# The level products of an RWKV-7 chunk on quarters of the PE array, one matmul for each batch half

## The chip, the cores and the metric

The kernel runs on one core of one Trainium2 chip. The metric is the device time of one execution in microseconds (us). Engines are TensorE (PE, with its weight loads listed as PEld), VectorE (DVE), ScalarE (ACT), GpSimd (POOL) and SyncE (SP, which here only issues transfers).

## The reference

Two stages follow each other: a linear-attention recurrence (RWKV-7 "goose") over 4 batches, 8 heads, 768 steps and head width 40, and a SwiGLU feed-forward block over the 3072 tokens of width 320 that come out of it.

```
state = 0                                   # per batch and head, 40 x 40
for t in range(768):
    y[t]  = r[t] @ state
    Sa    = state @ a[t]
    state = state * w[t] - outer(Sa, b[t]) + outer(v[t], k[t])

x  = y as (3072, 320);  xn = x / rms(x) * rms_g
out = (silu(xn @ w_gate) * (xn @ w_val)) @ w_out        # d_ff = 1536
```

Weights and rms_g of the feed-forward block are float64 in the inputs and are narrowed on the chip; all matmuls are in float32.

## The kernel before

The sequence is cut into 24 chunks of C = 32 steps. The 32 sequences (batch x head) lie as N = 8 slots by two column halves o by two partition halves i: a half of the 128 partitions (`half(i)`, 64 rows) belongs to one batch pair, `part(o)` is the first 40 rows of a half, and NI = 16 pairs (n, i) or (o, n) share a tile.

Within a chunk the recurrence is solved by doubling levels l = 1, 2, 4, 8, 16 (`LEVELS`). For each chunk there are four functions:

- `front(c)` loads w, a, k, b and v, turns them with PE, and builds level by level the decayed products T, the keys KN[l] and the lower triangular tile LT ("gramk" matmuls with 40 rows and 64 columns of weights).
- `inverse(c)` (for c < 4 `early_inverse`) inverts the triangle, in 31 pairs of DVE operations on tiles Yi and tmp, or by halves.
- `main(c)` solves for the chunk's values ("state", "lower" matmuls), updates the state ("update"), makes the scores of r against k and b ("score"), masks them into As, and computes y: a term from the old state ("y0") and one product for each level ("level"), which `down` adds into y after a scaling with T[l].
- `feed(g)`, after every second chunk, streams the narrowed weights of the feed-forward block in 12 slices (wf) and computes "h64", "h" and "out" matmuls with 256 to 320 moving columns.

`narrow_slice` prepares these weights during the first groups.

The operations are recorded as pieces (`Plan.add`) and issued in the order of the string ORDER, a list that was searched offline: each number is a piece's place among those not issued yet, and each "-" is a filler matmul on an identity tile (`plan.warm`, 151 of them, all in the first part of the kernel). PAIRS says which of three PSUM tiles each temporary (`plan.room()`) gets. So each engine's queue is a fixed sequence, and semaphores keep the dependencies. Nearly all DVE operations have line L444, all POOL and SP transfers L483, and PE's matmuls L486 (transposes L489), since one helper issues each kind; groups are told apart by the tiles' names.

The part that is changed is in `main`. The scores `sc` come out with the partitions of both batch halves filled. For each level j the tile `As[:, j]` holds the scores of that level's steps twice, once for each batch half i, and msi is zero where the partition half is not i:

```
As[:, j, :, i]  <-  sc * msi[:, j, i]        # [P, NI, 2, 16]
level: 16 matmuls  ps[part(o), slot(n)] = KN[l][all 128 rows, 40 cols].T @ As[all 128 rows, 32 cols]
```

So one matmul contracts over all 128 partitions and makes the 16 columns of both batch halves, which the zero blocks keep apart. Levels 16 and 8 share a PSUM temporary with y0, levels 4, 2 and 1 have one of their own.

Of the kernel before, what the change touches and what calls it, by code (L numbers as in the profile page):

```python
# [17 lines left out]
P = 128  # L18
# [15 lines left out]
85 83 84 76 58 78 86 74 73 59 60 75 5 89 61 88 77 4 43 6 201 7 87 334 90 44 8 214 213 53 62 9 - - - - - - - - 93 18 10  # L34
567 335 557 11 12 13 79 14 15 94 566 80 210 16 95 558 108 17 200 - - - 97 96 19 20 100 21 2 22 101 23 98 25 568 202 24
26 107 112 57 - - - - - 102 106 111 124 27 209 122 392 103 109 52 119 113 104 54 578 569 577 155 199 125 110 105 204
120 - - - - - - 114 203 118 117 121 559 211 598 589 562 46 131 129 132 45 560 212 597 563 588 561 123 115 136 586 384
133 134 - - - - - 126 130 116 47 564 3 145 216 394 383 135 336 128 137 48 144 143 141 91 587 219 142 51 570 127 1005
565 146 138 337 55 573 579 281 393 220 582 608 571 390 234 239 607 572 583 580 380 574 251 222 38 221 609 575 581 42 -
- - - - - - - 223 82 226 339 64 379 227 338 39 81 139 224 263 149 576 238 153 56 249 247 590 206 584 228 382 237 591  # L40
593 272 40 233 232 381 154 0 593 32 139 390 204 228 591 388 234 249 247 - - 324 235 35 31 27 244 229 146 147 259 281
245 258 149 34 325 594 36 33 270 155 243 62 605 584 598 230 - 239 40 214 599 601 242 628 64 49 91 627 602 30 626 1135
600 28 48 257 603 29 241 68 150 255 65 0 1347 194 0 194 84 173 0 - - - 182 540 200 0 184 1 186 542 540 0 506 0 457 469
849 199 455 242 111 97 110 112 96 51 61 439 460 458 122 50 243 0 0 255 242 0 709 104 470 242 120 246 259 708 57 247
458 456 0 257 718 256 470 242 0 716 265 487 486 0 268 0 0 265 101 473 0 262 277 0 273 0 236 0 260 0 269 0 242 461 - -
- - - - - 237 0 240 0 278 242 252 0 242 252 0 90 0 0 98 99 246 0 0 230 440 0 230 94 93 457 440 231 - - - - - - - - -
240 441 244 0 44 0 468 440 255 0 450 468 269 469 0 257 214 439 238 213 203 0 257 203 93 449 92 0 0 234 - - - - - - - -
245 437 0 250 262 0 464 246 247 436 260 245 446 258 259 469 244 - - 255 471 465 468 470 466 0 269 215 255 478 466 93
94 264 95 96 266 97 0 97 470 1 2 98 99 0 0 96 467 97 469 98 468 251 265 99 470 100 471 101 441 102 103 258 104 105 260
106 - - - - - - - - - - - 0 106 107 471 108 0 108 502 503 472 0 108 109 110 111 0 0 0 0 0 - - 13 0 16 562 572 146 571  # L50
561 147 14 142 143 374 15 13 355 - - - 25 386 358 0 358 386 388 16 25 387 389 390 70 79 17 391 28 191 147 355 356 80
148 149 359 0 68 28 2 29 149 0 149 34 150 29 151 187 24 25 31 152 33 153 188 391 393 32 154 35 390 392 358 0 0 152 40
187 153 27 154 155 156 33 157 158 159 160 161 34 162 36 163 164 37 165 41 391 38 42 392 39 394 561 166 395 393 552 0
42 559 549 548 395 209 0 549 560 42 165 210 43 44 211 427 428 395 - - - 565 166 45 167 557 168 0 565 566 168 739 0 522
693 534 526 124 - - 0 526 124 139 0 535 681 682 579 0 535 545 547 140 536 138 141 0 547 545 555 543 578 0 558 520 567
- - - - - - 518 378 0 696 378 380 381 695 518 120 685 526 - - - - - - 522 686 379 527 382 136 530 383 554 529 121 - -
141 540 523 565 539 537 142 538 524 - - - - 145 525 148 534 149 152 154 551 535 147 555 - - 157 146 550 536 150 155
151 556 165 552 153 564 160 691 161 692 0 163 161 689 162 165 1 0 546 676 0 510 45 46 560 47 424 511 2 1 0 0 555 554
44 45 563 509 421 432 436 435 422 437 433 571 508 996 995 434 444 572 442 441 0 45 572 442 585 577 0 838 45 572 445
577 46 828 827 837 587 573 589 446 575 47 598 48 601 11 846 588 574 444 443 613 597 0 11 370 835 599 48 0 584 607 367  # L60
478 595 568 - - 35 830 594 567 820 38 36 - 476 37 571 366 570 0 605 356 433 434 435 436 120 437 0 317 318 319 320 441
321 322 323 355 456 324 458 459 442 4 357 325 457 326 327 443 328 0 443 328 329 330 331 357 0 35 0 330 2 37 450 359 3
36 358 331 332 357 333 356 0 462 330 461 464 448 331 332 468 364 447 463 31 467 476 458 333 365 334 335 0 425 439 441
302 426 436 0 6 439 2 0 435 332 2 436 443 444 0 448 332 442 334 443 333 340 449 0 32 297 329 342 330 - 3 338 33 341
334 0 332 331 0 332 293 441 0 438 0 436 293 333 336 295 337 309 438 338 1 375 342 310 365 374 515 27 292 0 362 26 28
44 339 29 34 292 27 32 338 0 646 29 34 336 32 0 439 64 315 647 646 339 440 441 63 340 0 287 413 312 313 623 12 414 314
415 315 416 608 624 32 417 480 418 625 419 420 421 316 626 638 33 0 312 417 625 418 - - - - 476 313 601 602 600 610
812 419 420 421 822 258 422 423 0 313 810 423 625 637 2 0 819 2 0 254 473 420 421 645 310 422 0 - - - - - 310 422 3
313 33 0 28 626 307 419 639 627 420 637 308 0 637 20 635 420 647 21 421 23 422 613 648 819 38 22 809 423 39 659 24 611
3 612 36 818 424 651 808 621 425 25 660 426 - 616 249 427 0 427 3 25 58 57 428 28 47 0 428 429 28 430 3 431 0 26 25  # L70
614 484 31 27 617 627 0 458 216 400 590 600 401 0 12 582 32 401 583 25 0 397 579 21 - - - - - - - - - 588 29 28 30 591
22 453 428 398 605 23 0 591 23 429 602 24 609 0 24 397 588 602 1 604 398 429 430 2 399 427 0 584 - - - - - - - - - - -
- - - 4 397 0 25 397 4 0 393 394 21 23 27 28 395 598 24 424 607 0 21 38 35 395 37 396 24 2 424 47 397 398 399 400 25
401 3 28 402 403 588 0 28 3 0 584 26 27 585 25 598 600 422 31 400 399 401 424 599 28 595 427 429 52 0 568 397 396 399
567 394 405 578 401 12 0 398 397 570 0 381 367 402 0 1 569 576 381 501 570 0 509 0 648 574 381 497 403 382 399 402 0
706 399 400 419 715 403 0 655 715 401 705 402 0 402 783 657 403 703 655 404 0 711 566 700 655 565 712 564 3 563 358 8
360 0 3 639 403 0 403 3 0 400 401 402 712 403 355 0 710 968 406 350 724 715 1134 712 711 632 716 561 976 492 416 1133
663 729 634 977 562 563 717 713 986 978 665 564 565 566 975 567 568 714 569 985 570 571 967 722 572 723 - 0 400 403
726 402 572 401 573 0 726 738 736 573 739 574 664 575 737 576 577 3 723 578 751 579 760 580 747 581 582 633 583 584 0
584 585 3 634 586 636 587 635 734 588 633 0 746 588 - - - - - 403 757 589 722 590 3 404 591 592 593 594 595 596 408  # L80
597 598 599 600 601 602 603 714 409 410 0 727 401 728 711 402 600 712 601 0 408 712 725 721 0 417 723 600 601 3 602
401 735 737 0 741 602 735 721 0 739 0 0 330 10 196 313 342 197 198 324 20 199 200 201 202 203 0 203 340 338 204 325
339 4 324 206 205 335 5 6 0 335 336 346 343 345 344 228 0 0 227 0 200 341 343 226 344 342 3 235 13 625 234 202 232 229
8 233 204 203 230 201 231 227 348 4 349 228 350 351 352 353 354 355 356 0 0 351 3 0 351 7 352 16 353 3 354 355 8 356
357 358 359 360 361 362 0 359 5 360 361 6 0 355 6 356 357 358 359 218 16 360 361 220 362 223 363 227 224 364 225 228
365 229 0 365 536 366 367 527 368 369 524 225 370 16 371 372 525 195 229 534 373 230 0 195 249 536 230 231 525 232 541
250 0 399 533 203 0 541 730 371 231 540 372 373 0 371 229 543 254 539 372 230 200 373 726 544 393 374 445 551 255 375
554 394 231 376 567 377 565 378 0 736 395 554 231 541 735 232 539 555 733 378 567 379 579 565 743 233 380 540 381 4
563 734 575 382 588 383 744 236 386 234 384 576 587 319 385 235 5 320 6 548 549 544 396 397 545 552 400 551 399 0 386
397 561 560 545 546 402 0 557 0 398 401 557 553 399 518 519 0 564 571 524 551 665 525 566 570 567 400 438 550 565 579  # L90
# [278 lines left out]
def kernel(  # L369
# [108 lines left out]
    def blank(o, value):  # L478
        plan.add("POOL", "set", lambda at: nc.gpsimd.memset(o, value), [o], [])
# [70 lines left out]
    for j, l in enumerate(LEVELS):  # L550
        for i in range(2):
            pcopy(msi[half(i), j, i:i + 1].rearrange("p n (g l) -> p n g l", l=l), side(msk[half(i)], l, 1)[:, j:j + 1])
# [495 lines left out]
```

## Time and profile before

The time before is 1067.85 us, the median of 3 runs (1063.42, 1067.85 and 1081.36). The profiled execution took 1062.36 us; its span, from the first to the last instruction, is 1060.6 us.

| engine | busy us | share of the span | instructions |
|---|---|---|---|
| PE matmuls | 1009.5 | 95% | 23406 |
| PE weight loads | 829.3 | 78% | 23406 |
| DVE | 842.3 | 79% | 2861 |
| ACT | 468.1 | 44% | 1043 |
| POOL | 309.5 | 29% | 554 |

| what the change touches | count | mean ns of one |
|---|---|---|
| level matmuls from KN tiles, 128 rows x 40 columns, 32 moving | 3072 | 205 |
| level matmuls from kbn (level 1), same shape | 768 | 205 |
| masks As on DVE, 256 elements | 144 | 416 |
| masks As on DVE, 512 elements | 42 | 683 |
| masks As on ACT, 256 elements | 12 | 473 |
| adds of a level into y on DVE, 256 elements | 119 | 420 |

A busy time is the union of an engine's instructions, which overlap on PE. A row of a group gives the operation, tiles out<-in, shapes, count, then busy us and mean ns of one, then the idle time just before them and what ended it. A float32 matmul stands as two records, a transpose as one. In the forms of PE, "128*40" is rows by columns of the weights, and behind it the output's partitions by moving columns.

### The profile page before, as it was taken

How to read it: one execution, taken by the hardware profiler on the slowest of the kernel's cores; microseconds unless marked ns; L12 is line 12 of the kernel's file. 1: busy time of each engine (PE TensorE's matmuls, PEld its weight loads, DVE VectorE, ACT ScalarE, POOL GpSimd, SP SyncE). 2: the span in 40 equal slices, each digit the busy share in tenths (PEclk: the TensorE clock that was granted, in tenths of full speed). 3: DMA queues.
4: the chain of work that ended last, by engine and by line, in shares of the span. 5: the costliest groups of instructions: out<-in, count | busy, mean ns of one | idle time of the engine just before them, and what ended most of it. 6: DMA issues, size and time to landing. Idle time of an engine off the chain costs nothing.

```text
span 1060.6 us, 53494 instructions
## 1 busy us (share of the span) xinstructions
PE 1009.5 (95%) x23406; PEld 829.3 (78%) x23406; DVE 842.3 (79%) x2861; ACT 468.1 (44%) x1043; POOL 309.5 (29%) x554
## 2 busy tenths in 40 slices
PE   7868999999999999999999999999999999999997
PEld 6767777777888778787778778787777888787875
DVE  8978878776868988898898798989889899787411
ACT  6856666643543534434443444434344443431211
POOL 8824413120532241241233241340331331110000
PEclk9777998999999999999999999999999999999999
DMA  9965458766565483655565555574555555443252
GB/s 168 216 155 133 77 127 207 211 123 178 127 140 126 106 173 96 150 134 125 123 155 129 135 132 114 122 160 119 137 126 126 138 137 138 100 132 102 80 162 68
DMA packets 172457, 143.35 MB, mean 135 GB/s; under 512 B 125504, under 2 KB 143872, under 8 KB 172224
## 3 DMA queue, kind: packets, MB, share of 16 engines
q1 hardware_dynamic: 153856, 116.96, 42.9%
q0 software_dynamic: 16192, 22.64, 12.1%
q8 instruction: 184, 3.01, 1.2%
q10 hardware_dynamic: 2176, 0.33, 0.3%
q14 instruction: 49, 0.40, 0.1%
HBM read 123.86 MB, written 15.99 MB: 132 GB/s over the span
## 4 chain that ended last, share of the span: by engine, by line
PE 72%; DVE 8%; DMA 4%; ACT 3%; issue 3%; POOL 2%; SPq 1%; DVEq 0%; ACTq 0%; POOLq 0%
PE ps L486 50%; PE po L486 13%; PE ps L489 8%; DMA wf<-sW 2%; DVE LT L444 1%; DVE y L444 1%; DVE tmp L444 1%; POOL kbn L483 1%; DVE Yi L444 1%; DVE K L444 1%; SPq L483 1%; DMA sY<-Yi 1%; ACT VU L467 1%; PE po L1015 0%; DVE Ab L444 0%
## 5 line engine op out<-in xcount | busy, mean ns | idle before, releaser
L486 PE MATMUL ps<-xg,wf 128*128 128x256 f32 (+1 forms) x1728 | 353.5, 390 | 4.0 <-DVE xg L444 2.0
L486 PEld LDWEIGHTS ps<-xg,wf 128*128 128x128 f32 (+1 forms) x1728 | 261.4, 188 | 57.2 <-issue 15.0
L486 PE MATMUL po<-wf,hT 128*128 128x320 f32 x576 | 183.1, 449 | 0.1
L464 ACT ACTIVATE sg<-ps 128x256 f32<-128x256 f32 x144 | 53.6, 382 | 228.2 <-PE ps L486 224.9
L444 DVE TENSOR_TENSOR tmp<-Yi,M 128x60 f32<-128x60 f32 (+24 forms) x620 | 130.7, 211 | 19.1 <-DMA M<-sB 5.9
L444 DVE TENSOR_TENSOR Yi<-Yi,tmp 128x60 f32<-128x60 f32 (+24 forms) x620 | 129.7, 209 | 12.7
L483 POOL DMA_DIRECT2D VU<-in_v_dram x92 | 53.2, 584 | 274.1 <-PE ps L486 141.8
L486 PEld LDWEIGHTS po<-wf,hT 128*128 128x128 f32 x576 | 102.5, 191 | 35.7 <-issue 4.1
L444 DVE TENSOR_TENSOR hT<-ps,sg 128x256 f32<-128x256 f32 x144 | 59.7, 420 | 67.2 <-ACT sg L464 66.4
L444 DVE TENSOR_TENSOR K<-K,T 128x512 f32<-128x512 f32 (+1 forms) x192 | 93.4, 496 | 8.3 <-PE ps L486 5.8
L486 PEld LDWEIGHTS ps<-Ab,K 40*64 40x64 f32 x4608 | 77.2, 138 | 28.1 <-issue 10.5
L467 ACT COPY K<-K 128x256 f32<-128x256 f32 (+1 forms) x168 | 71.7, 443 | 58.4 <-PE ps L486 39.2
L486 PE MATMUL ps<-Ab,K 40*64 40x56 f32 x4608 | 87.2, 224 | 9.7 <-issue 3.8
L444 DVE TENSOR_TENSOR As<-ps,msi 128x256 f32<-128x256 f32 (+1 forms) x186 | 78.9, 476 | 14.4 <-PE ps L486 13.8
L467 ACT COPY KN<-ps 128x640 f32<-128x640 f32 x96 | 66.1, 690 | 53.5 <-PE ps L489 23.3
L483 POOL DMA_DIRECT2D kbn<-in_b_dram x92 | 53.3, 583 | 96.7 <-PE ps L486 94.3
L486 PEld LDWEIGHTS ps<-As,KN 128*40 128x40 f32 x3072 | 66.5, 124 | 15.7 <-issue 10.4
L483 POOL DMA_DIRECT2D kbn<-in_k_dram x92 | 53.6, 585 | 82.7 <-PE ps L486 82.6
L486 PE MATMUL ps<-As,KN 128*40 128x32 f32 x3072 | 73.2, 205 | 3.1 <-issue 2.5
L483 POOL DMA_DIRECT2D wn<-in_w_dram x92 | 51.6, 567 | 62.7 <-DVE tmp L444 24.1
L444 DVE TENSOR_TENSOR y<-y,ps 128x256 f32<-128x256 f32 x119 | 50.0, 420 | 16.2 <-PE ps L486 13.7
L444 DVE COPY_PREDICATED LT<-near,ps 128x384 f32<-128x384 uint32 (+2 forms) x72 | 52.2, 725 | 2.6 <-PE ps L486 2.0
(133 smaller groups left out, 1546.0 us busy)
## 6 DMA issues: line engine op xcount, KB each, us to landing
wf<-sW SPq DMA_DIRECT2D x144, 480.0 KB, 3.9
M<-sB SPq DMA_DIRECT2D x80, 128.0 KB, 4.1
rn<-in_r_dram SPq DMA_DIRECT2D x24, 160.0 KB, 5.4
sW<-ex SPq DMA_DIRECT2D x16, 240.0 KB, 3.4
out_dram<-o SPq DMA_DIRECT2D x48, 80.0 KB, 4.2
kbn<-in_k_dram POOLq DMA_DIRECT2D x92, 40.0 KB, 3.9
kbn<-in_b_dram POOLq DMA_DIRECT2D x92, 40.0 KB, 4.1
wan<-in_a_dram POOLq DMA_DIRECT2D x46, 80.0 KB, 4.9
```

The lines of the kernel that those rows point to most:

```text
L444: plan.add("DVE", kind, lambda at: fn(at(o), *m(at)), [o], aps(*args))
L464: plan.add("ACT", "act", lambda at: nc.scalar.activation(at(o), at(a), f, **kw), [o] + aps(acc), [a])
L467: plan.add("ACT", "copy", lambda at: nc.scalar.copy(at(o), at(a)), [o], [a])
L483: plan.add(by, "dma", lambda at: queue.dma_start(out=o, in_=i), [o], [i])
L486: return o, lhsT, rhs, lambda at: nc.tensor.matmul(at(o), lhsT, rhs, start=start, stop=stop, skip_group_check=True)
L489: return o, i, ident, lambda at: nc.tensor.transpose(at(o), i, ident)
```

## The change

As gets one score per element and no zero blocks ([P, 5, NI, 16]); the mask msi is one row of 16 for each level. A level is now 32 matmuls: for each slot n, batch half i and column half o, the 64 rows of `half(i)` with 40 columns of weights and 16 moving columns, written to `part(o)` of PSUM half i. The PSUM temporaries are laid out by i accordingly, and `down` reads them through one more dimension. ORDER and PAIRS are new strings (151 fillers, as before, and 499 temporaries).

```diff
-    msi = const.tile([P, len(LEVELS), 2, 16], FP32, name="msi")
+    msi = const.tile([P, len(LEVELS), 16], FP32, name="msi")
...
-    blank(msi, 0.0)
     for j, l in enumerate(LEVELS):
-        for i in range(2):
-            pcopy(msi[half(i), j, i:i + 1].rearrange("p n (g l) -> p n g l", l=l), side(msk[half(i)], l, 1)[:, j:j + 1])
+        pcopy(msi[:, j:j + 1].rearrange("p n (g l) -> p n g l", l=l), side(msk, l, 1)[:, j:j + 1])
...
-    As_ = Turns(1, [P, len(LEVELS), NI, 2, 16], "As")
+    As_ = Turns(1, [P, len(LEVELS), NI, 16], "As")
...
             if G == 1 and c < LATE:
-                for i in range(2):
-                    scale(As[:, j, :, i], sc.rearrange("p o n t -> p (o n) t")[:, :, 16:C], msi[:, j, i, 0:1])
-            elif G == 1 or l == 1:
-                tt(As[:, j], sc.rearrange("p o n t -> p (o n) t")[:, :, None, 1 if l == 1 else 16:C:2 if l == 1 else 1].to_broadcast((P, NI, 2, 16)),
-                   msi[:, j:j + 1].to_broadcast((P, NI, 2, 16)), MUL)
+                scale(As[:, j], sc.rearrange("p o n t -> p (o n) t")[:, :, 16:C], msi[:, j, 0:1])
             else:
-                for i in range(2):
-                    tt(As[:, j, :, i].rearrange("p n (g l) -> p n g l", g=G),
-                       side(sc.rearrange("p o n t -> p (o n) t")[:, :, 0:C], l, 1),
-                       msi[:, j:j + 1, i].rearrange("p n (g l) -> p n g l", g=G).to_broadcast((P, NI, G, l)), MUL)
+                tt(As[:, j].rearrange("p n (g l) -> p n g l", g=G), side(sc.rearrange("p o n t -> p (o n) t")[:, :, 0:C], l, 1),
+                   msi[:, j:j + 1].rearrange("p n (g l) -> p n g l", g=G).to_broadcast((P, NI, G, l)), MUL)
...
-            pe("level", [mm(ps[part(o), slot(n)], z["KN"][LEVELS[j]][:, kn_at(LEVELS[j], n, o)],
-                              As[:, j, o * N + slot(n)].rearrange("p i t -> p (i t)")) for n in range(N) for o in range(2)])
+            pe("level", [mm(ps[part(o), i, slot(n)], kn(z, LEVELS[j], i, n, o), As[half(i), j, o * N + slot(n)]) for n, i, o in each])
...
-            tt(yr, yr, ps.rearrange("p n (i g l) -> p (n i) g l", i=2, g=G), ADD)
+            yr = side(y, l, 1).rearrange("p (n i) g l -> p n i g l", i=2)
+            tt(yr, yr, ps.rearrange("p i n (g l) -> p n i g l", g=G), ADD)
...
-        yl = ps[:, :, N * C:].rearrange("p f (n t) -> p f n t", n=N)
+        yl = ps[:, :, N * C:].rearrange("p i (f n t) -> p f i n t", f=2, n=N)
...
-            copy(y[:, :, 16:], yl[:, 0].rearrange("p n (i l) -> p (n i) l", i=2))
+            copy(y[:, :, 16:].rearrange("p (n i) l -> p n i l", i=2), yl[:, 0].rearrange("p i n l -> p n i l"))
...
-        yl = plan.room().rearrange("p u (f n t) -> p (u f) n t", n=N, f=2)
+        yl = plan.room().rearrange("p i (f n t) -> p f i n t", f=4, n=N)
```

In the instruction orders of the two built programs, PE has 12,311 matmuls before and 14,231 after, DVE 2,549 two-operand operations before and 2,477 after, and each queue the same number of transfers (SP 696, POOL 460, ACT 8).

## The prediction

> **What bounds the kernel now.** I read the page first.
>
> ```profile
> PE 1009.5 (95%) x23406; PEld 829.3 (78%) x23406; DVE 842.3 (79%) x2861; ACT 468.1 (44%) x1043; POOL 309.5 (29%) x554
> PEclk9777998999999999999999999999999999999999
> q8 instruction: 184, 3.01, 1.2%
> PE 72%; DVE 8%; DMA 4%; ACT 3%; issue 3%; POOL 2%; SPq 1%; DVEq 0%; ACTq 0%; POOLq 0%
> ```
>
> TensorE (PE) is busy 95% and is 72% of the chain that ended last; its granted clock is full from 100 us on, so prices per instruction are constant there. The table of stages shows where it has air:
>
> ```profile
> 0.00:50.00 50.00, 38.89 (x744) 34.91 (x744) 44.10 (x122) 37.24 (x75) 44.98 (x98) 0.86 0.91 188
> 300.00:400.00 100.00, 98.23 (x2157) 80.25 (x2156) 86.67 (x306) 43.73 (x102) 30.16 (x51) 1.00 0.59 135
> 800.00:900.00 100.00, 98.79 (x2408) 81.11 (x2407) 90.44 (x313) 42.88 (x95) 28.03 (x49) 1.00 0.55 131
> ```
>
> Columns: stretch, its length, busy us of PE, PEld, DVE, ACT, POOL, clock, DMA. Until about 240 us PE idles (39 of 50 us) and runs filler matmuls; after that it is 98% busy, so there a PE nanosecond added is a nanosecond added. Next the groups of instructions, for what is changed:
>
> ```profile
> L486 PE MATMUL ps<-As,KN 128*40 128x32 f32 x3072 | 73.2, 205 | 3.1 <-issue 2.5 <-DVE tmp L444 0.7
> L486 PE MATMUL ps<-VU,KN 64*40 64x40 f32 x1536 | 20.5, 204 | 1.3 <-issue 1.3
> L444 DVE TENSOR_TENSOR As<-ps,msi 128x256 f32<-128x256 f32 x144 | 54.1, 416 | 4.8 <-PE ps L486 4.2 <-ACT As L470 0.4
> L444 DVE TENSOR_TENSOR As<-ps,msi 128x512 f32<-128x512 f32 x42 | 28.4, 683 | 9.6 <-PE ps L486 9.6
> ```
>
> A float32 matmul leaves two records (a pair of weight load and matmul each). Last, PE's timeline, for the price of one piece from its start to the next start:
>
> ```profile
> 447.43 0.57 PE L486 MATMUL ps<-Ab,K 40*64 40x56 f32 x24 [0.53 <-issue]
> 447.82 0.81 PE L486 MATMUL ps<-VU,KN 64*40 64x40 f32 x64
> 448.56 1.99 PE L486 MATMUL ps<-xg,wf 128*128 128x256 f32 x8
> 450.39 1.04 PE L489 MATMUL ps<-ident,VU 128*104 128x128 f32 x8
> 451.36 0.57 PE L486 MATMUL ps<-Ab,K 40*64 40x56 f32 x24
> 452.54 0.81 PE L486 MATMUL ps<-Ab,K 40*64 40x56 f32 x40 [0.61 <-issue]
> ...
> 503.85 1.42 PE L486 MATMUL ps<-As,KN 128*40 128x32 f32 x64
> 505.19 0.78 PE L486 MATMUL ps<-ST,aP 40*32 40x40 f32 x64
> ```
>
> Two things are to be seen. First, prices: two levels (64 pairs) take 1.34 us; one takes 0.735 us wherever it stands alone and three take 1.962, so a level is 0.613 us (19.2 ns a pair) plus 0.12 us once where the array goes over to another tiling. The state update, 64 pairs on quarters of the array, takes 0.74 us, and 0.636 where a piece of the same tiling follows: 9.9 ns a pair and 0.11 us for the change. y0 (40 rows, 32 moving columns) gives 0.634, so the width of the moving side hardly matters.
>
> Second, the stops marked "issue". Between the two above lie 24+64+8+8+24 = 128 pairs, 256 instructions. The queue of kind instruction brought 184 packets, 3.01 MB: 16 KB each, and PE's 47,125 instructions over 184 are 256. So PE stops where the next block of 256 has not come. I followed all 184 packets: every such stop lies at a multiple of 256 instructions after the first; in dense stretches the packet starts 0.7 to 2.7 us after PE entered the block before, takes 1.1 us, and PE goes on 1.3 us after its end. So a block of quick instructions lasts at least about 3.3 us; only four of 143 took less (1.55 to 2.93 us), behind longer instructions, where the packet had started earlier, up to 2.7 us before PE got there. After 240 us these stops add up to about 11 us.
>
> **The change part by part.** *Level products.* 120 pieces (5 levels, 24 chunks) go from 16 matmuls on all rows to 32 on half the rows with 16 moving columns. 64 pairs at y0's or the update's 9.9 ns are 0.634 us against 0.613: +0.021 x 120 = +2.5 us. Bounds: the 16x16 product of the early inverse (64 pairs, 0.606 us) gives -0.8 us; no overlap of quarters is a rival below. The instruction orders of the two programs show 531 changes of tiling before and 556 after, since levels now stand in 70 groups and not 51: 25 x 0.11 = +2.8 us.
>
> *Instruction refills.* 1,920 more matmuls are 7,680 more instructions, 30 more blocks, and the new ones are the quickest there are. A typical new block is 240 instructions of levels and 16 of feed: 120 x 9.9 ns + 8 x 216 ns + 0.2 = 3.1 us; the same mixture before was 120 x 19.2 ns + 1.73 + 0.2 = 4.2 us, over the 3.3 us. I walked both orders in blocks of 256 with the prices above (gram 15, score 15, state and lower 9.4, feed 216, 110 and 269, transposes 89 to 109 ns a pair). In the part after 240 us, before has 16 of 143 blocks under 3.3 us, short by 8.8 us together, and 25 under 3.5 us, short by 12.8; the measured 11 lies between. The changed order has 56 of 167 under 3.3 us, short by 39.9, and 67 under 3.5, short by 52.5. The difference is 31 to 40 us; I take +30, at the lower end, because a block behind long matmuls gets its refill asked for early. Bounds: counting only what lies under 3.0 us, 26.4 - 4.8 = +22; counting to 4.0 us, 92.6 - 29.9 = +63. In the early part it is 21.6 - 8.5 = +13 at 3.3 us, but PE idles there anyway: +5, bounds 0 and 13.
>
> The Trainium skill (Runtime: NRT & Kernel Launch, section Instruction fetch mechanics) has the same 16 KiB blocks of 256 instructions, and says that crossing a boundary is mostly hidden. By that rule this term is nothing and the sum is about 1061 us; the stops of 0.53 and 0.61 us above speak against it for dense runs.
>
> *Masks on DVE and ACT.* Before: 144 x 416 ns + 42 x 683 ns = 88.6 us summed (82.5 us of busy time), after 114 x 416 = 47.4: at least -35 us on DVE; ACT loses 6 of 12 scalings at 473 ns. This lies beside PE's work after 240 us. Early, DVE work on masks is on the chain: 1.4% of the chain's first 300 us, 4.2 us, and per chunk 3.2 us of masks become 1.7. I take -3, bounds 0 and -9 (all of 6 x 1.5).
>
> *Late waits of PE for DVE and ACT.* With the refill stops aside, PE's time after 240 us is 32 us over my walk; only 8 us of PE's idle rows there name DVE or ACT. Less DVE work takes some: -4, bounds 0 and -9.
>
> *At nothing:* the adds of a level into y read the same 256 elements through one more dimension; the nearest row with that pattern, y<-ps,T, takes 420 ns like y<-y,ps now. The mask tile is prepared by 5 copies on POOL, not 10 and a blanking (-2 us at 30 us), beside the loads that fill POOL's queue there. No wait is added on POOL or SP; all DMAs are the same in number, and behind a later PE they are only later by as much.
>
> *Sum* against the profiled execution's own 1062.4 us (span 1060.6 and 1.8 around it, 5.5 us under the median of 1067.85): 1062.4 + 2.5 + 2.8 + 30 + 5 - 3 - 4 = 1095.7, forecast 1096 us.
>
> **The rivals.** *The refills hide (1061 us).* The 32 us of other late delay and the new stops fall together, and PE comes out only with its own work: 1062.4 + 5.3 - 7. For it: 30 us is no more than that delay, and the new order has levels in 70 groups between other work. Against: the stops come on top of the walk today.
>
> *DVE was what held PE (faster, 1042 us).* If half of the 32 us late and 9 us early are chains through DVE (masks, y), 35 us less work ends them: 1062.4 + 5.3 - 16 - 9.6. It decides as soon as a mask or an add comes in time for the level or turn that waits for it and no block is late. For it: DVE is 87 to 90% busy in the late stages. Against: PE's idle rows name it for few us, and PE is 98% busy.
>
> *Refills take longer when they come thick (1136 us).* With 4 us a block: 1062.4 + 5.3 + 63 + 13 - 7. For it: some packets started 2 to 3.5 us late in busy DMA stretches. Against: the measured 11 us fits 3.3 to 3.5.
>
> *Quarters don't overlap at 16 columns (1132 us).* If a pair costs 19.2 ns still, 120 x 32 x 19.2 ns = +74 us, and the blocks are slow enough for their refills: 1062.4 + 74 + 2.8 - 7. Against it stand the update and y0. The Trainium skill has this rule (TensorEngine Tiling (Array Packing), section Instruction Overhead): a matmul costs about 60 cycles whatever its small width, so halving a small dimension gains nothing.
>
> **How the numbers follow.** Forecast 0.59 (own range 1078 to 1118), refills hidden 0.20, DVE 0.09, longer refills 0.08, no overlap 0.04. The range 1050 to 1130 leaves out most of DVE's case and the two highest. A measurement of this kernel tells about 2% from no change: 1046 and 1089 us. Of the forecast's 0.59 I put 0.46 over 1089 and 0.13 within, and the two high cases, 0.12, over it: slower 0.58; with the hidden case within 0.33; faster 0.09.
>
> **What would show it.** Right: about 214 instruction packets; a level alone at 0.63 to 0.75 us; DVE busy near 807 us; "issue" before PE pieces several times as much as now, on multiples of 256 instructions, most of it inside levels. Wrong: stops no more than now (then the refill term fails), a level near 1.2 us (quarters don't overlap), or PE's busy time falling with the span (DVE held it).

## The result and the profile after

The changed kernel takes 1179.73 us at the median (1165.24, 1179.73 and 1187.16), against 1067.85 before. Without the slowest run of each (1187.16 and 1081.36 us, which fell in a slower state of the chip) it takes 1.100 times as long, 95% interval 1.069 to 1.131. The profiled execution took 1179.73 us, its span is 1177.5, 116.9 more than before. Forecast 1096, range 1050 to 1130: the sign was right and the size was not.

From the page of the changed kernel, the lines that answer to those shown of before (busy times; granted clock in 40 slices; the queue that brings instructions; the chain that ended last):

```profile
PE 1065.8 (91%) x27246; PEld 866.2 (74%) x27246; DVE 809.4 (69%) x2789; ACT 466.0 (40%) x1037; POOL 309.7 (26%) x548
PEclk9877789999999999987999999988999999899899
q8 instruction: 214, 3.51, 1.3%
PE 76%; DVE 9%; issue 7%; ACT 4%; DMA 2%; POOL 2%; SPq 0%; DVEq 0%; ACTq 0%; POOLq 0%
```

PE is busy 91% now, not 95%; "issue", the time in which it waits for nothing that the profile shows, is 7% of the chain against 3%; and the row of the clock, which was all nines after 186 us, has eights and a seven in it to the end. The groups of the level products and of their masks:

```profile
L483 PE MATMUL ps<-As,KN 64*40 64x16 f32 x6144 | 85.3, 193 | 30.0 <-issue 28.4
L441 DVE TENSOR_TENSOR As<-ps,msi 128x256 f32<-128x256 f32 x114 | 43.0, 417 | 19.9 <-PE ps L483 19.3
```

Ahead of the KN levels PE sat 28.4 us on "issue", ahead of the old ones 2.5. The table of stretches (columns as in the prediction: PE, PEld, DVE, ACT, POOL, then clock and DMA), first of before, then of after:

```profile
0.00:250.00 250.00, 220.30 (x5442) 187.67 (x5442) 200.39 (x637) 155.76 (x330) 101.34 (x198) 0.91 0.69 160
250.00:1060.00 810.00, 789.23 (x17965) 641.65 (x17964) 641.87 (x2225) 312.32 (x713) 208.18 (x356) 1.00 0.53 128
```

```profile
0.00:250.00 250.00, 209.82 (x5758) 181.38 (x5760) 182.14 (x575) 147.63 (x310) 100.43 (x192) 0.86 0.61 150
250.00:1177.00 927.00, 855.95 (x21492) 684.78 (x21488) 627.23 (x2216) 318.34 (x728) 209.28 (x356) 0.96 0.45 115
```

After 250 us the clock falls from 1.00 to 0.96 as a mean, and PE idles 71 us (927.00 - 855.95) where it idled 21. PE's waits over the whole span, before and then after (total, times, longest):

```profile
PEld ps L486 <- issue: 62.4, 157, 2.0
PE ps L486 <- issue: 16.9, 25, 1.8
```

```profile
PEld ps L483 <- issue: 133.2, 213, 3.2
PE ps L483 <- issue: 64.1, 62, 3.2
```

No other releaser grew by more than a few us. How the two things meet is seen in PE's timeline of after; "x126" counts records, two for a float32 matmul:

```profile
766.80 1.99 PE L483 MATMUL ps<-xg,wf 128*128 128x256 f32 x8
768.84 1.40 PE L483 MATMUL ps<-As,KN 64*40 64x16 f32 x126
...
772.85 0.79 PE L483 MATMUL ps<-As,kbn 64*40 64x16 f32 x61 [2.58 <-issue]
773.58 0.86 PE L483 MATMUL ps<-ST,aP 40*32 40x40 f32 x64
774.37 0.31 PE L483 MATMUL ps<-As,KN 64*40 64x16 f32 x3
776.60 2.32 PE L483 MATMUL ps<-As,KN 64*40 64x16 f32 x125 [1.92 <-issue]
778.85 2.50 PE L483 MATMUL po<-wf,hT 128*128 128x320 f32 x4
781.28 1.29 PE L483 MATMUL ps<-VU,LT 32*32 32x40 f32 x64
782.50 1.63 PE L486 MATMUL ps<-ident,ST 104*104 104x104 f32 x8
```

```profile
767.10:770.50 3.40, 3.14 (x139) 2.52 (x137) 2.12 (x7) 0.39 (x1) 0.00 (x0) 1.00 0.67 169
770.50:773.90 3.40, 1.05 (x97) 1.02 (x99) 2.01 (x5) 0.00 (x0) 0.26 (x1) 1.00 0.10 21
773.90:777.30 3.40, 1.48 (x89) 1.28 (x81) 0.00 (x0) 0.00 (x0) 3.40 (x7) 0.50 0.30 56
777.30:780.70 3.40, 3.40 (x101) 2.64 (x93) 1.63 (x6) 0.00 (x0) 0.96 (x2) 0.50 0.27 50
780.70:784.10 3.40, 3.40 (x75) 2.73 (x74) 1.73 (x8) 0.44 (x1) 0.00 (x0) 0.50 0.47 151
```

A level stops for 2.58 us in its middle, the next one for 1.92. In the 3.4 us of the first stop PE works 1.05 us; the three windows behind it run at clock 0.50. There 125 records of a level take 2.32 us (126 took 1.40 at full clock), and four "out" records 2.50 (1.26 at 785 us, at full clock again).

From the trace I took two sums for every kernel. *Late stops*: the times after 245 us in which PE starts nothing, at a multiple of 256 instructions, and which end about 1.4 us behind the end of the instruction packet that was due. They are counted from where the next matmul would have started; the idle rows of the profile begin at the modelled end of the last matmul, about 0.2 us later, and give some 52 us at these places in after and 9 in before. *Late half clock*: time at clock 0.5 after 245 us, without the last 8 us of the span. Both sums are of the one profiled execution of a kernel. Before has 9.7 us of stops (18, at 142 crossings) and no late half clock. After has 62.8 us of stops (58, at 170 crossings) and 81.6 us of half clock, in 14 stretches of 3.4, 6.8 or 10.2 us.

### The profile page after: what moved, and what is told of

The parts are those of the page before. It is cut to its first block, busy times and chain, and to the rows that moved or that the text cites. A ratio compares the mean times of both kernels' runs of the same rounds, so it can differ in the third digit from the quotient of the medians.

```text
span 1177.5 us, 61083 instructions
## 1 busy us (share of the span) xinstructions
PE 1065.8 (91%) x27246; PEld 866.2 (74%) x27246; DVE 809.4 (69%) x2789; ACT 466.0 (40%) x1037; POOL 309.7 (26%) x548
## 4 chain that ended last, share of the span: by engine, by line
PE 76%; DVE 9%; issue 7%; ACT 4%; DMA 2%; POOL 2%; SPq 0%; DVEq 0%; ACTq 0%; POOLq 0%
PE ps L483 52%; PE po L483 13%; PE ps L486 10%; DVE LT L441 1%; PE po L1004 1%; DVE tmp L441 1%; DVE K L441 1%; DMA wf<-in_moe_w_out_dram 1%; ACT KN L464 1%; DVE Yi L441 1%; DMA wan<-in_a_dram 1%; ACT VU L464 1%; ACT K L464 1%; POOL kbn L480 1%; DVE y L441 0%
## 5 line engine op out<-in xcount | busy, mean ns | idle before, releaser
L483 PE MATMUL ps<-xg,wf 128*128 128x256 f32 (+1 forms) x1728 | 371.6, 406 | 8.6 <-issue 5.8
L483 PEld LDWEIGHTS ps<-xg,wf 128*128 128x128 f32 (+1 forms) x1728 | 270.4, 196 | 66.3 <-issue 22.0
L483 PE MATMUL po<-wf,hT 128*128 128x320 f32 x576 | 187.6, 457 | 0.8 <-issue 0.7
L483 PEld LDWEIGHTS ps<-As,KN 64*40 64x40 f32 x6144 | 76.6, 128 | 49.0 <-issue 43.5
L483 PE MATMUL ps<-As,KN 64*40 64x16 f32 x6144 | 85.3, 193 | 30.0 <-issue 28.4
L441 DVE TENSOR_TENSOR As<-ps,msi 128x256 f32<-128x256 f32 x114 | 43.0, 417 | 19.9 <-PE ps L483 19.3
```

What stands on the lines that cost most here:

```text
L441: plan.add("DVE", kind, lambda at: fn(at(o), *m(at)), [o], aps(*args))
L483: return o, lhsT, rhs, lambda at: nc.tensor.matmul(at(o), lhsT, rhs, start=start, stop=stop, skip_group_check=True)
```

## The experiments

The theory, T1: refills stop PE, and the stops and the small matmuls leave the array so little to do that its clock is halved. Rivals: the new order, the lighter masks, or a clock that falls for another reason.

| kernel | ratio to before (95%) | median us | span, clock of the profiled run | late stops us | late half clock us |
|---|---|---|---|---|---|
| before | 1 | 1067.85 | 1060.6, 0.979 | 9.7 | 0 |
| after | 1.100 (1.069 to 1.131) | 1179.73 | 1177.5, 0.936 | 62.8 | 81.6 |
| quarters_old_order | 1.139 (1.128 to 1.149) | 1214.93 | 1209.4, 0.906 | 79.6 | 142.9 |
| after_old_order | 1.134 (1.128 to 1.140) | 1210.03 | 1208.0, 0.905 | 78.8 | 153.2 |
| full_rows | 1.026 (1.020 to 1.032) | 1095.19 | 1092.5, 0.969 | 14.3 | 10.2 |
| half_levels | 1.014 (1.008 to 1.020) | 1082.30 | 1081.2, 0.960 | 21.8 | 20.4 |
| fill_wide | 1.111 (1.101 to 1.120) | 1188.76 | 1183.1, 0.964 | 26.5 | 10.2 |
| fill_small | 1.148 (1.141 to 1.156) | 1230.80 | 1228.1, 0.922 | 21.5 | 129.5 |
| light_masks_only | 0.991 (0.986 to 0.995) | 1061.50 | 1066.2, 0.974 | 9.0 | 3.4 |

Each ratio is to runs of before beside it: 1068.36 us for the four kernels in the middle, 1074.59 for the last three. The intervals of half_levels and light_masks_only reach no further than 2% from before.

**Only PE's part, in the old order.** The masks with their zero blocks stay, and so do all pieces and their order. (The cut shows the matmuls; PSUM's layout and the reads in `down` follow as in the change.)

```diff
-            pe("level", [mm(ps[part(o), slot(n)], z["KN"][LEVELS[j]][:, kn_at(LEVELS[j], n, o)],
-                              As[:, j, o * N + slot(n)].rearrange("p i t -> p (i t)")) for n in range(N) for o in range(2)])
+            pe("level", [mm(ps[part(o), i, slot(n)], kn(z, LEVELS[j], i, n, o), As[half(i), j, o * N + slot(n), i]) for n, i, o in each])
```

> Only the PE part of the change: 32 matmuls on quarters of the array for a level, with the masks, the zero blocks (now unread) and the order of the kernel before. Theory 1 (PE runs out of instructions, and the clock falls after such stops): blocks of 256 instructions after 240 us are short of 3.65 us by 89 us together, against 63 in the changed kernel and 17 before, because the old order sets levels side by side; the time is then above the changed kernel's 1180 us, 1200 to 1240. Theory 2 (the new order brings the waits): with the old order back the loss is gone but for the dearer levels and changes of tiling, 1065 to 1075 us. Theory 3 (the lighter masks change what DVE delivers when): as theory 2, since the masks are the old ones.

1214.93 us. The quarters by themselves cost more than the whole change; the line of the late stretch is that of after, only more so:

```profile
250.00:1209.00 959.00, 871.24 (x21569) 702.12 (x21567) 659.83 (x2293) 322.29 (x736) 208.77 (x357) 0.92 0.45 111
```

**The whole change, in the old order.** ORDER and PAIRS are those of before, without the mask pieces that fell away.

```diff
-ORDER = (the new string)
+ORDER = (the string of before, each number mapped to the same piece)
```

> The changed kernel's operations in the order of the kernel before (removed masks left out of it, PSUM temporaries as before). Theory 1: as with the old masks, short blocks of 89 us after 240 us, 1200 to 1240 us, and within 10 us of the kernel that has the quarters with the old masks, since 35 us of DVE work are not what PE waits for. Theory 2: 1060 to 1075 us. A theory in which DVE's work counts has it some 20 us or more under the kernel with the old masks.

1210.03 us: within 5 us of the run above, so the lighter masks change little while the stops rule; the new order takes off some 30 us, by 16 us fewer stops and 72 us less half clock, though at the price found below these two alone would be worth about 45.

**Full rows in the new order.** Each level has 16 matmuls again, and half of PSUM's places are not written, so this kernel does not compute the level terms.

```diff
-            pe("level", [mm(ps[part(o), i, slot(n)], kn(z, LEVELS[j], i, n, o), As[half(i), j, o * N + slot(n)]) for n, i, o in each])
+            pe("level", [mm(ps[part(o), n % 2, slot(n)], z["KN"][LEVELS[j]][:, kn_at(LEVELS[j], n, o)], As[:, j, o * N + slot(n)]) for n in range(N) for o in range(2)])
```

> The changed kernel with its own order and light masks, but a level is 16 matmuls over all 128 rows with 16 moving columns (the two batch halves' products are added up and only one PSUM half of each slot is written, so the level terms of y are left out in effect). Instructions are as many as before. Theory 1: short blocks after 240 us fall to 13 us from 63, about 184 refills, clock near 0.98: 1055 to 1075 us. Theory 2: the order stays, so 1160 us or more. A theory in which only DVE's relief matters: 1030 us or less.

1095.19 us: 85 us of the loss are gone with the 1,920 matmuls, and stops and half clock with them. It stays 20 us above what I expected; the last run below takes that up. The late stretch:

```profile
250.00:1092.00 842.00, 809.84 (x18130) 650.53 (x18128) 616.34 (x2182) 314.02 (x719) 208.74 (x356) 0.99 0.50 125
```

**Every second quarter left out.** Quarters, but as few matmuls as before, so half of the level products are missing.

```diff
-            pe("level", [mm(ps[part(o), i, slot(n)], kn(z, LEVELS[j], i, n, o), As[half(i), j, o * N + slot(n)]) for n, i, o in each])
+            pe("level", [mm(ps[part(o), i, slot(n)], kn(z, LEVELS[j], i, n, o), As[half(i), j, o * N + slot(n)]) for n, i, o in each if i == n % 2])
```

> The changed kernel with every second of the quarter matmuls of a level left out (16 matmuls on quarters, 16 moving columns; half of the level products is left out). Tiling, order and masks stay; PE's walk is 38 us shorter and the instructions are as many as before. Theory 1: short blocks of 21 us after 240 us, 1025 to 1050 us, clock 0.96 or more. A theory in which it is the quarter tiling as such that lowers the clock or stalls PE, not the number of instructions: half of the loss stays, 1100 us or more.

1082.30 us, 32 us above the 1025 to 1050 that I expected and under the 1100 of the rival. A level alone is 0.30 us at the least where it was 0.61, so 120 x 0.31 = 37 us less matmul work than full_rows; it is only 13 us faster. So work on the quarters is not what costs, the count of instructions is; but what PE saves comes back in part, as 7.5 us more stops and 10 us more half clock, and as waits for others: PE is busy 92% of this span. Its late stretch:

```profile
250.00:1081.00 831.00, 786.15 (x18131) 623.82 (x18129) 615.97 (x2184) 314.60 (x721) 209.38 (x356) 0.99 0.51 127
```

**Wide and small fillers where blocks are short.** Time is put in where stops would be, once with the full array and once with a sixteenth of it.

```diff
+    plan.fill = lambda: nc.tensor.matmul(po_[0:P, 0, DM:].rearrange("p (u v) -> p u v", u=2), ident[0:P, 0:P],
+                                         ident[0:P, None, 0:96].to_broadcast((P, 2, 96)), start=False, stop=False, skip_group_check=True)
```

(fill_small has 32 in place of each P, and the same 191 places.)

> The changed kernel with 191 filler matmuls more (an identity of 128 rows and columns against 192 moving columns, about 0.33 us each by the 0.22 us of the 128-column fillers), put after 240 us into 55 places, where my walk of PE's order in blocks of 256 instructions finds a block too short for its refill. By the walk they and their tiling changes add 69 us to PE and take the refill stops after 240 us from about 63 to about 15 us, so on these two sums alone it gets 21 us slower: about 1200 us. Theory T1: the granted clock is halved after a window of some 3.4 us in which the array did little, and the stops and the small level products make such windows; the fillers are full-array work, so half clock after 240 us falls from 82 us to under 25 us and gives back some 30 to 40 us: 1150 to 1180 us, mean clock 0.955 or more. Rival T2: the clock falls for another reason (the load of the whole chip, or the time since the start): half clock stays at 60 us or more and the time is 1190 to 1215 us.

> The same 191 fillers at the same places, but with 32 rows and 32 columns of weights (a sixteenth of the array), the same 192 moving columns and so the same time on PE. T1 in its narrow form (what counts is how much of the array works, by rows and columns): they don't count, half clock after 240 us stays at 50 us or more, 1185 to 1215 us, at least 15 us over the kernel with wide fillers. T1 in its wide form (what counts is that PE streams at all): the clock holds as with the wide fillers, within 10 us of that kernel.

1188.76 and 1230.80 us. The fillers' own records (shortest, median and longest ns, first and last start), first of the wide, then of the small kernel:

```profile
L1005 PE MATMUL po<-ident x382: 326/326/430, 280.9 to 1127.9; 128*128 128x192 f32 x191
```

```profile
L1005 PE MATMUL po<-ident x382: 321/321/523, 280.7 to 1171.4; 32*32 32x192 f32 x191
```

And the late stretch of each, in the same order:

```profile
250.00:1183.00 933.00, 895.37 (x21872) 724.61 (x21868) 625.81 (x2215) 317.69 (x727) 209.40 (x356) 0.99 0.45 114
```

```profile
250.00:1228.00 978.00, 943.75 (x21870) 732.45 (x21866) 626.20 (x2213) 317.34 (x727) 209.30 (x356) 0.93 0.43 109
```

The same number of fillers, equally long at full clock, at the same places: the wide ones hold the clock at 0.99, the small ones leave it at 0.93, lower than after's 0.96, though PE is busy 96 to 97% in both. T1 holds in its narrow form: what counts here is not that PE streams, but how much of the array works; whether it is rows, columns or both, the pair does not tell. The small fillers bring 18 more changes of tiling (639 against 621), 2 us at 0.11. The small kernel came out above its 1185 to 1215, with more half clock than after. The pair prices it: 119 us more half clock (129.5 - 10.2), with 5 us fewer stops, make the span 45.0 us longer: (45.0 + 5.0) / 119 = 0.42 us lost per us of half clock. Of the 45.0 us, 4.5 arose before the first filler (the fourth chunk's update starts at 217.8 and at 222.3 us); without them the price is 0.38.

The wide kernel came out above its 1150 to 1180, because 26.5 us of stops were left and not 15. With the walk's 69 us for the fillers and their tiling changes, and the rest measured, it closes: 1177.5 + 69 - 36 of stops - 71 x 0.42 = 1180 against a span of 1183.1. As a way out it fails: the fillers cost what the stops and the clock gave back.

**Only the masks.** The kernel before with the light masks; the moving side gives each score twice, so this kernel does not compute the level terms either. (The cut shows the matmuls only.)

```diff
-                              As[:, j, o * N + slot(n)].rearrange("p i t -> p (i t)")) for n in range(N) for o in range(2)])
+                              As[:, j, o * N + slot(n), None].to_broadcast((P, 2, 16))) for n in range(N) for o in range(2)])
```

> The kernel before with only the masks of the changed one: one score per element and no zero blocks, each level still 16 matmuls on all 128 rows with 32 moving columns (the 16 scores given twice; so the level terms of the two batch halves are mixed, which leaves them out in effect). The order is that of before without the pieces that fell away. DVE has about 35 us less work, PE the same matmuls and 184 refills. If the changed order by itself costs the 27 us by which the changed kernel with full rows lay over before: 1055 to 1068 us here, at best 5 us under before. If it is the light masks or what follows them: 1080 to 1100 us. If DVE had held PE: under 1050 us.

1061.50 us, 1.0% less than before (0.5 to 1.4%), with DVE at 808.9 us as in after. The late stretch:

```profile
250.00:1066.00 816.00, 794.39 (x18044) 645.43 (x18044) 614.64 (x2167) 313.58 (x714) 208.88 (x356) 1.00 0.51 127
```

So 33 us less of DVE work are worth about 10 us, and DVE did not hold PE. And full_rows, which has the same masks and the same number of level matmuls in the changed order, stands at 1.026: the changed order, with its PSUM layout, costs 26 us by the two spans and 38 by the ratios where the quarters are not there. Of that, 5 us are stops, 41 more tiling changes (572 against 531) at 0.11 are 4.5, and 7 us more half clock some 3. The rest is spread: the fourth chunk's update starts 10 us later (214 against 204 us), the last chunk's 21 us later. What in the order does it is not settled.

No run pointed to a computing version that beats before: the masks' 10 us hang on the quarters, which cost more than ten times that.

## Why the prediction was wrong in size

**Right.** 214 packets; DVE at 809.4 us (807 foretold); a level alone 0.634 us at the least, two 1.247, three 1.861, so a pair on quarters costs its 9.9 ns and the +2.5 and +2.8 us stand. The rival in which quarters do not overlap falls with them. The rule of the Trainium skill that the prediction set beside it (TensorEngine Tiling (Array Packing), section Instruction Overhead) is about the width of the moving side, and the traces agree with that part: on all 128 rows a further level takes 0.613 us with 16 columns (full_rows) and as much with 32 (before). It is no rule against quarters, where a pair costs 9.9 ns and not 19.2. The masks' -3 and the late waits' -4 are close to the 10 us that light_masks_only shows. The stops are where they were foretold, on multiples of 256, many inside levels.

**The refill term was too small: +30, measured +53** (and +4 for +5 early). I took the lower end because 9.7 us of stops in before fitted a shortest block of 3.3 to 3.5 us. In after a stopped block took 4.1 us at the median from its start to the next one's, and 4.4 in before. The same walk with 3.65 us a block, a value taken with after's trace at hand, comes within about 10 us of six kernels, four of which had not yet been run:

| late shortage at 3.65 us, and late stops, us | before | after | quarters_old_order | after_old_order | full_rows | half_levels |
|---|---|---|---|---|---|---|
| walk | 16.8 | 63.0 | 89.1 | 89.2 | 13.4 | 21.5 |
| trace | 9.7 | 62.8 | 79.6 | 78.8 | 14.3 | 21.8 |

For fill_wide the walk had 15 us, and 26.5 came. So the form of the step was right and its one constant was too small: it had been fitted to a kernel in which few blocks come near it. The bound of +63 lay nearer than +30. The Trainium skill's rule that the crossing is mostly hidden (Runtime: NRT & Kernel Launch, section Instruction fetch mechanics) fits before, where 18 of 142 late crossings stop PE, and is no guide to after, where 58 of 170 do, for 62.8 us; the rival built on it falls.

**The step that failed outright: "its granted clock is full from 100 us on, so prices per instruction are constant there".** This was read from before and carried over to after. Even of before it is not exact: its row has an eight in the slice from 159 to 186 us, and the trace has half clock from 176 to 183 us. Later the profiled execution of before has none; windows like 770.5 to 773.9 us above are new. At 0.38 to 0.42 us each, 81.6 us of late half clock are 31 to 34 us, and no term, bound or rival of the prediction held them. The Trainium skill has the mechanism (TensorE: Matmul & The Clock Gate, Part 1): a free-running window of about 3.4 us, and half rate after a window in which PE idles. The lengths of 3.4, 6.8 and 10.2 us agree with it. But here the window ahead of a drop was not idle: in the 3.4 us ahead of after's 14 drops PE was busy for 1.04 to 2.40 us, and ahead of 15 of fill_small's 17 for 3.0 us or more, of six of them throughout. So an idle window is not needed for the drop, and the measurement decides.

**A smaller misreading:** "PE idles (39 of 50 us)" takes the busy time for the idle time. In that row PE idles 11 us, and over the first 250 us 30 (250.00 - 220.30), so the early part of before was less slack than the prediction took it to be.

**The sum with measured terms:** 1062.4 + 5.3 + 53 + 4 + 34 = 1159, against 1179.7; with 10 off for the masks, 1149. So 21 to 31 us are left. A good part of them lies early: the fourth chunk's update starts at 203.2 us in before and at 223.6 in after (217.8 and 222.3 in the two fill kernels, which are the same program up to there), 15 to 20 us later where the prediction had +5, and half clock before 245 us rose from 44 to 68 us. From that update to the last chunk's, before takes 788.7 us and after 886.9: 98 more, of which the late terms (53 + 34 and most of 5.3) make up 90 or so. The remainder is no more than what the changed order costs in full_rows; as the cause of that is open, this is a balance and not a proof. The order was worth 30 us where quarters made the stops (after against after_old_order), and cost about as much where they did not: a term that the prediction did not have, since it costed the order by tiling changes and stops alone.

## What to carry to other kernels

When small matmuls are halved in size and doubled in number, count instructions before array time: walk the order in blocks of 256, and take the limit from a kernel in which many blocks are really stopped (3.65 us fitted here; 4.1 us was the median of the stopped blocks), not from one that hardly meets it. Then ask of each 3.4-us window how much of the array still works: a stop of 2 us is paid twice when the clock comes down behind it. A clock row full of nines says that the present work held the clock, not that the next kernel's will.

## What was not expected of the hardware

In these kernels the clock went by how much of the array works and not by PE being busy: 382 records of 321 ns on 32 rows and 32 columns left 129.5 us of late half clock, as many of 326 ns on 128 x 128 left 10.2. And the packet itself is the smaller part of a refill: in the stopped blocks of after (medians) it starts 1.7 us behind the crossing into the block ahead and takes 1.0 us, and PE goes on 1.4 us behind its end.
